# Talking-heads attention and a gated feed-forward: in each step, three blocks of four (two of three) go into the first head mixing as split fp32r pairs, instead of two (one)

## The chip, the cores and the metric

The kernel runs on one core of a Trainium2 chip. The metric is the time of one execution on the device in microseconds; the time given for a kernel is the median of several executions. The trace is that of one further execution, taken with the hardware profiler.

## The reference

```python
scores = scale * np.matmul(q, k.transpose(0, 1, 3, 2))      # batch 4, heads 12, seq 448, dim 64
scores = np.einsum('bhij,hg->bgij', scores, w_pre)          # first mixing of the heads
scores = scores - np.max(scores, axis=-1, keepdims=True)
attn = np.exp(scores)
attn = attn / (np.sum(attn, axis=-1, keepdims=True) + 1e-09)
attn = np.einsum('bhij,hg->bgij', attn, w_post)             # second mixing
out = np.matmul(attn, v).astype(np.float32)
...
h = x @ w_in                                                # x: (1792, 768), w_in: (768, 2048)
g = np.where(pos, h, np.where(neg, 0.0, (h + beta) ** 2 / (4.0 * beta)))
return (g @ w_out).astype(np.float32)
```

## The kernel before

The program has two parts. The attention fills the first half of the span, the feed-forward the second; the change touches only the attention.

**Tiles, blocks, groups.** The 448 query rows of a batch are cut into tiles of 120, 120, 120 and 88 rows, 16 tiles in all. `scores` writes the scores of a tile, for all 12 heads, to `ssb` (row, head, key). A block is 10 query rows times 12 heads, so 120 rows of 448 keys: `load_s` gathers it by a DMA from `ssb` into a tile `s` of its own (tag `s10`, 8 buffers). In this form the mixing of the heads is one matrix product with a 120x120 block-diagonal matrix. A tile of 120 rows has 12 blocks in 3 groups of four; the tile of 88 rows has 9 blocks in 3 groups of three. There are 48 groups and 180 blocks.

**A step.** The loop over n handles one group per step, and the order of each engine's work is the order of the code (there is no scheduler). In step n the code issues the loads of group n+1; `pre` of the blocks of group n (first mixing into a PSUM tile `ps_l`, on PE); `row_max` (DVE); the split of a block of the next group; `exps` (ACT, tile `e`); `norm` (DVE, then `wr` on POOL); the remaining splits; part of the conversion of the feed-forward's weights (`wt`, `wk` on ACT and DVE, an add on POOL); `post` of group n-1 (second mixing on PE into `ps_a`, which ACT copies to `aT`); in some steps the transposes of the next keys (`trans_k`, `ps_k`) and queries (`trans_q`, `ps_t`); `pv` (`ps_x`, copied to `xo`); the scores of a later tile (`ps_s`, copied to `ssb` by ACT and DVE); and further loads. The first of group n-1's `post` is written inside the loop of `exps`, ahead of the fourth; ACT copies the other three after it. Steps 0 to 47 are meant where a step is numbered.

**Two forms of the first mixing.** A block that was not split goes into `pre` as one fp32 product (line 200; the trace shows two instructions for one). A block that was split goes in as three fp32r products (line 198): high part with high weights, high with low, low with high. `split` makes the high part `sh` by a cast (DVE, line 187) and the low part `sl` by a subtraction (DVE, line 188).

**PSUM.** `ps_l`, `ps_a`, `ps_k`, `ps_t` (after the first tiles), `ps_x` and the second pair of `ps_s` all come from one pool of 6 buffers, which are handed out in turn: a new tile takes the buffer of the tile six before it, and PE waits until that one has been read.

**Loads.** All these loads are issued from SP's queue, in the order of the code. In a group of four they are issued as blocks 1, 3, 0, 2; in a group of three as 1, 0, 2.

Of the kernel before, what the change touches and what calls it, by code (L numbers as in the profile page):

```python
# [10 lines left out]
F32R = mybir.dt.float32r  # L11
# [3 lines left out]
AF = mybir.ActivationFunctionType  # L15
# [7 lines left out]
def tile_talking_heads_moe(  # L23
# [11 lines left out]
    nc = tc.nc  # L35
    B, H, S, D = q.shape
# [5 lines left out]
    KM = IB * H  # L42
# [17 lines left out]
    ap_ = s_att.enter_context(tc.tile_pool(name="att", bufs=2))  # L60
# [12 lines left out]
    for b in range(B):  # L73
        for i0 in range(0, S, QT):
            n = min(QT, S - i0)
            tiles.append((b, i0, n, -(-n // IB)))
    blocks = []
    groups = []
# [6 lines left out]
    NG = len(groups)  # L85
# [89 lines left out]
    def load_s(m):  # L175
        t, o, ni, c = blocks[m]
        n, nb = tiles[t][2:]
        x = ap_.tile([KM, S], F32, tag="s10", name="s10", bufs=8)
        nc.sync.dma_start(out=x[:ni * H], in_=ssb[t][o:n:nb])  # L179
        s10[m] = x  # L180

    def split(m):
        k = blocks[m][2] * H
        x = s10.pop(m)
        hi = ap_.tile([KM, S], F32R, tag="sh", name="sh", bufs=2)
        lo = ap_.tile([KM, S], F32R, tag="sl", name="sl", bufs=2)
        nc.vector.tensor_copy(out=hi[:k], in_=x[:k])
        nc.vector.tensor_tensor(out=lo[:k], in0=x[:k], in1=hi[:k].bitcast(F32), op=ALU.subtract)
        s10[m] = (hi, lo)

    def pre(m):

        k = blocks[m][2] * H
        lps[m] = ps_l.tile([KM, S], F32, tag="l", name="ps_l")
        x = s10.pop(m)
        if isinstance(x, tuple):
            for j, (w, y) in enumerate(((wpre_h, x[0]), (wpre_l, x[0]), (wpre_h, x[1]))):
                nc.tensor.matmul(out=lps[m], lhsT=w[:k], rhs=y[:k], start=(j == 0), stop=(j == 2))  # L198
        else:
            nc.tensor.matmul(out=lps[m], lhsT=wpre[:k], rhs=x[:k], start=True, stop=True)  # L200

    def row_max(m):
        nm = ap_.tile([KM, 1], F32, tag="nm", name="nm", bufs=8)
        nc.vector.tensor_reduce(out=nm, in_=lps[m], axis=AX.X, op=ALU.max, negate=True)  # L204
        lps[m] = (lps[m], nm)

    def exps(m, j, sm):
        ps, nm = lps.pop(m)
        e = ap_.tile([KM, S], F32, tag="e", name="e", bufs=8)
        nc.scalar.activation(out=e, in_=ps, func=AF.Exp, bias=nm, accum_out=sm[:, j:j + 1])  # L210
        ex[m] = e

    def norm(ms, sm):
        k = len(ms)
        rs = ap_.tile([KM, 4], F32, tag="rs", name="rs", bufs=3)
        nc.vector.tensor_scalar_add(out=rs[:, :k], in0=sm[:, :k], scalar1=1e-9)
        nc.vector.reciprocal(out=rs[:, :k], in_=rs[:, :k])  # L217
        for j, m in enumerate(ms):
            ni = blocks[m][2]
            w = ap_.tile([KM, H, IB], F32, tag="wr", name="wr", bufs=8)  # L220
            nc.gpsimd.tensor_scalar_mul(out=w[:, :, :ni], in0=wpost[:, :, :ni], scalar1=rs[:, j:j + 1])  # L221
            wr[m] = w

    def post(m):
        t, o, ni, c = blocks[m]
        if o == 0:
            aT[t] = ap_.tile([KP, KC, H, QT], F32, tag="aT", name="aT")
        ps = ps_l.tile([KP, KC, H * IB], F32, tag="l", name="ps_a")
        e, w = ex.pop(m), wr.pop(m)
        for r in range(KC):  # L230
            nc.tensor.matmul(out=ps[:, r, :ni * H], lhsT=e[:, r * KP:(r + 1) * KP],  # L231
                             rhs=w[:, :, :ni], start=True, stop=True)
        nc.scalar.activation(out=aT[t][:, :, :, c:c + ni],  # L233
                             in_=ps[:, :, :ni * H].rearrange("q r (h i) -> q r h i", h=H), func=AF.Copy)
# [242 lines left out]
    with tc.manual_schedule():  # L477
# [41 lines left out]
        for m in groups[0]:  # L519
# [7 lines left out]
            out=wpre.rearrange("p (i g) -> p i g", g=H),  # L527
# [3 lines left out]
            out=wpost, in0=wrep[:, 1, :].unsqueeze(2).to_broadcast([KM, H, IB]),  # L531
# [56 lines left out]
        def convs(goal):  # L588
            while conv and nconv - len(conv) < goal:
                conv.popleft()()  # L590

        for n in range(NG + 2):
            if n == NE:
                s_qk.close()
                pool['fp'] = ctx.enter_context(tc.tile_pool(name="ffn", bufs=2, side="right",
                                                            reuse_waits="tile"))
                pool['ps_h'] = ctx.enter_context(tc.tile_pool(
                    name="ps_h", bufs=2, space=PSUM, side="right", reuse_waits="tile"))
            if n == NG - 1:
                s_ss.close()  # L600
                pool['fw'] = ctx.enter_context(tc.tile_pool(name="ffw", bufs=2, side="right",
                                                            reuse_waits="tile"))
            share = nconv / (NE - 1)
            ms = groups[n] if n < NG else ()
            old = list(groups[n - 1]) if 0 < n <= NG else []
            if n + 1 < NG:
                for m in (*groups[n + 1][1::2], *groups[n + 1][::2]):
                    load_s(m)
            if ms:
                sm = ap_.tile([KM, 4], F32, tag="sm", name="sm", bufs=3)  # L610
            for m in ms:
                pre(m)
            nxt = list(groups[n + 1][1::2]) if n + 1 < NG else []
            for m in ms:
                row_max(m)
            if nxt:
                split(nxt.pop(0))
            for j, m in enumerate(ms):
                if j == 3:
                    post(old.pop(0)) if old else None  # L620
                exps(m, j, sm)
            if ms:
                norm(ms, sm)
            for m in nxt:
                split(m)
            convs(share * (n + 0.4))
            for m in old:
                post(m)
            for f in at.pop(n, ()):
                f()  # L630
            for t, g in vis2.pop(n, ()):
                pv(t, g)
            for f in [scores(t, hps) for t, hps in vis.pop(n, ())]:
                f()
            for f in late.pop(n, ()):
                f()
            convs(share * (n + 1))
            if n == NG:
                h = ffn1(0)
# [77 lines left out]
```

## Time and profile before

| | |
|---|---|
| median of the runs | 946.18 us (944.99 to 948.36) |
| the profiled execution | 944.17 us |
| its span in the trace | 942.4 us |
| mean granted TensorE clock | 0.998 |
| PE matmul busy | 926.5 us, 98% |
| DVE / ACT / POOL busy | 609.4 / 542.2 / 179.7 us |

The span runs from the first to the last instruction; the time of the execution has 1.8 us more. A busy share is a mean over both parts of the program, whose limits differ.

### The profile page before, as it was taken

What the parts mean: (1) busy time and instruction counts of PE and PEld (TensorE: products, weight loads), DVE (VectorE), ACT (ScalarE), POOL (GpSimd) and SP (SyncE); (2) the same over time, 40 slices, a digit from 0 to 9 for tenths busy, and PEclk for the clock granted to TensorE, in tenths of its full rate; (3) what the DMA queues carried; (4) which work ended last, traced back from release to release, by engine and by line L of the source; (5) the groups of instructions that cost most, each with busy time, mean ns of one, the idle gap of its engine ahead of it and who ended that gap; (6) DMA issues with size and microseconds to landing.
All of it is one profiled execution on the core that took longest, in us unless ns stands there. A gap on an engine that the chain in (4) does not pass through costs nothing.

```text
span 942.4 us, 17968 instructions
## 1 busy us (share of the span) xinstructions
PE 926.5 (98%) x6734; PEld 781.4 (83%) x6734; DVE 609.4 (65%) x1113; ACT 542.2 (58%) x1146; POOL 179.7 (19%) x253
## 2 busy tenths in 40 slices
PE   7989999999999999999999999999999999999998
PEld 6668888888887888888888888888888888888997
DVE  4678768787778868765556675655445555445774
ACT  4767777766786777776655563533334433334553
POOL 0243334342434234331202230000000000000000
PEclk9999999999999999999999999999999999999999
DMA  6966756776678756744554540210000200000100
GB/s 110 235 194 182 209 177 207 244 207 178 200 220 221 214 169 205 221 171 145 153 196 151 184 140 1 76 37 1 12 12 12 85 1 1 11 1 20 55 1 34
DMA packets 118362, 115.21 MB, mean 122 GB/s; under 512 B 61701, under 2 KB 107269, under 8 KB 118277
## 3 DMA queue, kind: packets, MB, share of 16 engines
q1 hardware_dynamic: 115492, 113.38, 40.0%
q10 hardware_dynamic: 2784, 0.69, 0.5%
q8 instruction: 54, 0.88, 0.4%
q14 instruction: 32, 0.25, 0.1%
HBM read 55.85 MB, written 19.66 MB: 80 GB/s over the span
## 4 chain that ended last, share of the span: by engine, by line
PE 95%; DMA 3%; SPq 1%; DVE 0%; ACT 0%; issue 0%
PE o L458 25%; PE ps_h L419 25%; PE ps_a L231 15%; PE ps_x L247 9%; PE ps_l L200 8%; PE ps_s L155 6%; PE ps_l L198 5%; DMA s<-ssb 2%; PE ps_t L138 1%; PE ps_k L121 1%; DMA qraw<-in_q_dram 1%; SPq L179 0%; DMA k<-in_k_dram 0%; DVE kl L128 0%; SPq L110 0%; SPq L101 0%
## 5 line engine op out<-in xcount | busy, mean ns | idle before, releaser
L221 POOL TENSOR_SCALAR wr<-wpost,rs 120x120 f32<-120x120 f32 x180 | 113.3, 645 | 304.5 <-DVE rs L217 257.0
L231 PEld LDWEIGHTS ps_a<-wr,e 120*112 120x112 f32 x1440 | 154.3, 177 | 6.7 <-issue 4.9
L231 PE MATMUL ps_a<-wr,e 120*112 120x120 f32 (+1 forms) x1440 | 155.2, 266 | 0.0
L210 ACT ACTIVATE e<-ps_l,nm 120x448 f32<-120x448 f32 x180 | 112.8, 632 | 54.6 <-DVE nm L204 54.0
L419 PE MATMUL ps_h<-xh,wil 128*128 128x512 f32 (+1 forms) x384 | 139.5, 363 | 0.0
L419 PE MATMUL ps_h<-xl,wih 128*128 128x512 f32 (+1 forms) x384 | 139.2, 362 | 0.0
L419 PE MATMUL ps_h<-xh,wih 128*128 128x512 f32 (+1 forms) x384 | 139.2, 362 | 0.0
L458 PE MATMUL o<-woh,gh 128*128 128x512 f32 (+1 forms) x444 | 114.6, 339 | 0.0
L458 PE MATMUL o<-wol,gh 128*128 128x512 f32 (+1 forms) x444 | 114.1, 339 | 0.0
L433 ACT ACTIVATE a<-ps_h,c 128x512 f32<-128x512 f32 (+1 forms) x64 | 40.6, 634 | 127.6 <-PE ps_h L419 127.5
L458 PE MATMUL o<-woh,gl 128*128 128x512 f32 (+1 forms) x444 | 114.0, 338 | 0.0
L434 DVE TENSOR_TENSOR mx<-ps_h,a 128x512 f32<-128x512 f32 (+1 forms) x64 | 40.0, 625 | 110.4 <-ACT a L433 110.3
L204 DVE TENSOR_REDUCE nm<-ps_l 120x1 f32<-120x448 f32 x180 | 104.1, 619 | 10.5 <-PE ps_l L200 8.0
L200 PE MATMUL ps_l<-s,wpre 120*120 120x448 f32 x196 | 94.7, 567 | 6.4 <-DMA s<-ssb 6.4
L233 ACT ACTIVATE aT<-ps_a 112x480 f32<-112x480 f32 x180 | 95.8, 590 | 2.4 <-PE ps_a L231 2.1
L437 ACT ACTIVATE gh<-mx 128x512 fp32r<-128x512 f32 (+1 forms) x63 | 36.6, 581 | 90.3 <-DVE mx L435 90.3
L458 PEld LDWEIGHTS o<-woh,gl 128*128 128x128 f32 x444 | 75.0, 189 | 11.5
L247 PE MATMUL ps_x<-aT,v 112*64 112x120 f32 (+1 forms) x1536 | 83.8, 262 | 0.0
L458 PEld LDWEIGHTS o<-wol,gh 128*128 128x128 f32 x444 | 75.5, 188 | 9.9
L458 PEld LDWEIGHTS o<-woh,gh 128*128 128x128 f32 x444 | 75.7, 188 | 9.6
L419 PEld LDWEIGHTS ps_h<-xl,wih 128*128 128x128 f32 x384 | 72.4, 189 | 12.1
L419 PEld LDWEIGHTS ps_h<-xh,wih 128*128 128x128 f32 x384 | 72.4, 189 | 11.5
(83 smaller groups left out, 1459.1 us busy)
## 6 DMA issues: line engine op xcount, KB each, us to landing
s<-ssb SPq DMA_DIRECT2D x172, 210.0 KB
wraw<-in_moe_w_in_dram SPq DMA_DIRECT2D x32, 384.0 KB
raw<-in_moe_w_out_dram SPq DMA_DIRECT2D x20, 384.0 KB
wid<-wt SPq DMA_DIRECT2D x32, 192.0 KB
wi<-wid SPq DMA_DIRECT2D x16, 384.0 KB
v<-in_v_dram SPq DMA_DIRECT2D x12, 448.0 KB
out_dram<-osb SPq DMA_DIRECT2D x14, 384.0 KB
wraw<-in_moe_w_out_dram SPq DMA_DIRECT2D x12, 384.0 KB
```

Of the source, the lines that this page charges most:

```text
L155: nc.tensor.matmul(out=ps[s][:n], lhsT=qt[t][x][r, hp, :n], rhs=kt[b, hp][y][r, :], start=(m == 0), stop=(m == 2))
L198: nc.tensor.matmul(out=lps[m], lhsT=w[:k], rhs=y[:k], start=(j == 0), stop=(j == 2))
L200: nc.tensor.matmul(out=lps[m], lhsT=wpre[:k], rhs=x[:k], start=True, stop=True)
L204: nc.vector.tensor_reduce(out=nm, in_=lps[m], axis=AX.X, op=ALU.max, negate=True)
L210: nc.scalar.activation(out=e, in_=ps, func=AF.Exp, bias=nm, accum_out=sm[:, j:j + 1])
L221: nc.gpsimd.tensor_scalar_mul(out=w[:, :, :ni], in0=wpost[:, :, :ni], scalar1=rs[:, j:j + 1])
L231: nc.tensor.matmul(out=ps[:, r, :ni * H], lhsT=e[:, r * KP:(r + 1) * KP], rhs=w[:, :, :ni], start=True, stop=True)
L233: nc.scalar.activation(out=aT[t][:, :, :, c:c + ni], in_=ps[:, :, :ni * H].rearrange("q r (h i) -> q r h i", h=H), func=AF.Copy)
L247: nc.tensor.matmul(out=ps[s * D:(s + 1) * D, m, :n], lhsT=vt[b, g][:, 2 * m + s, r * D:(r + 1) * D], rhs=a[:, r, 4 * g + 2 * m + s, :n], s ...
L419: nc.tensor.matmul(out=ps[:, :n], lhsT=w[:, kk, :], rhs=x[:, :n], start=(c == 0), stop=(c == last))
L433: nc.scalar.activation(out=a[:, :n], in_=ps[:, :n], func=AF.Relu, scale=0.5, bias=c05)
L458: nc.tensor.matmul(out=o[bank][:, c0:c0 + ne], lhsT=g[:, t * 128:(t + 1) * 128], rhs=w[:, e0:e0 + ne], start=(f == 0 and m == 0 and c0 == ...
```

## The change

The blocks that are split are now all of a group but its first: blocks 1, 2 and 3 of four (before: 1 and 3), blocks 1 and 2 of three (before: 1). The low part no longer has a tile of its own but is written over the scores in their `s` buffer; `sh` has 4 buffers instead of 2. Block 3's cast is issued from ACT instead of DVE, its subtraction stays on DVE. The loads are issued as blocks 1, 2, 3, 0 (of three: 1, 2, 0), so block 0, the one that goes into the fp32 product, comes last. Group 0 is mixed without splits in both kernels.

```diff
-    def split(m):
+    def split(m, act=False):
         k = blocks[m][2] * H
         x = s10.pop(m)
-        hi = ap_.tile([KM, S], F32R, tag="sh", name="sh", bufs=2)
-        lo = ap_.tile([KM, S], F32R, tag="sl", name="sl", bufs=2)
-        nc.vector.tensor_copy(out=hi[:k], in_=x[:k])
+        hi = ap_.tile([KM, S], F32R, tag="sh", name="sh", bufs=4)
+        lo = x.bitcast(F32R)
+        if act:
+            nc.scalar.activation(out=hi[:k], in_=x[:k], func=AF.Copy)
+        else:
+            nc.vector.tensor_copy(out=hi[:k], in_=x[:k])
         nc.vector.tensor_tensor(out=lo[:k], in0=x[:k], in1=hi[:k].bitcast(F32), op=ALU.subtract)
...
-                for m in (*groups[n + 1][1::2], *groups[n + 1][::2]):
+                for m in (*groups[n + 1][1:], groups[n + 1][0]):
                     load_s(m)
...
-            nxt = list(groups[n + 1][1::2]) if n + 1 < NG else []
+            nxt = list(groups[n + 1][1:]) if n + 1 < NG else []
...
+            if nxt:
+                split(nxt.pop(0))
             for m in nxt:
-                split(m)
+                split(m, act=True)
```

On PE, the first mixing of group 2 (step 2), from the last product of the scores ahead of it to the second mixing behind it. The number of an `s` tile rises in the order in which the loads are issued. Before:

```order
L155 MATMUL ps_s_519<-kl_201,qh 120x448
L200 MATMUL ps_l<-s_425,wpre 120x448
L198 MATMUL ps_l<-sh,wpre_h 120x448
L198 MATMUL ps_l<-sh,wpre_l 120x448
L198 MATMUL ps_l<-sl,wpre_h 120x448
L200 MATMUL ps_l<-s_427,wpre 120x448
L198 MATMUL ps_l<-sh,wpre_h 120x448
L198 MATMUL ps_l<-sh,wpre_l 120x448
L198 MATMUL ps_l<-sl,wpre_h 120x448
L231 MATMUL ps_a<-wr,e 112x120 x16
```

The same place of the changed kernel:

```order
L155 MATMUL ps_s_523<-kl_201,qh 120x448
L203 MATMUL ps_l<-s_428,wpre 120x448
L201 MATMUL ps_l<-sh,wpre_h 120x448
L201 MATMUL ps_l<-sh,wpre_l 120x448
L201 MATMUL ps_l<-s_422,wpre_h 120x448
L201 MATMUL ps_l<-sh,wpre_h 120x448
L201 MATMUL ps_l<-sh,wpre_l 120x448
L201 MATMUL ps_l<-s_424,wpre_h 120x448
L201 MATMUL ps_l<-sh,wpre_h 120x448
L201 MATMUL ps_l<-sh,wpre_l 120x448
L201 MATMUL ps_l<-s_426,wpre_h 120x448
L234 MATMUL ps_a<-wr,e 112x120 x16
```

The third block's fp32 product has become three fp32r ones, and the tile that PE needs first is the fourth that is loaded (`s_428` of 422, 424, 426, 428) where it was the third (`s_425` of 421, 423, 425, 427).

On ACT, step 7, from its exponentials to the copy of `ps_x`. Before:

```order
L210 ACTIVATE e,sm<-ps_l,nm 120x448 x3
L233 ACTIVATE aT<-ps_a 112x48x10
L210 ACTIVATE e,sm<-ps_l,nm 120x448
L282 ACTIVATE wt<-wraw 128x384
L288 ACTIVATE wk<-wraw 128x384
L233 ACTIVATE aT<-ps_a 112x48x10 x3
L140 ACTIVATE qh<-ps_t 128x360
L254 ACTIVATE xo<-ps_x 128x240
```

The same place of the changed kernel:

```order
L213 ACTIVATE e,sm<-ps_l,nm 120x448 x3
L236 ACTIVATE aT<-ps_a 112x48x10
L213 ACTIVATE e,sm<-ps_l,nm 120x448
L188 ACTIVATE sh<-s_1234 120x448
L285 ACTIVATE wt<-wraw 128x384
L291 ACTIVATE wk<-wraw 128x384
L236 ACTIVATE aT<-ps_a 112x48x10 x3
L140 ACTIVATE qh<-ps_t 128x360
L257 ACTIVATE xo<-ps_x 128x240
```

The cast of the next group's block 3 stands between the last exponential and the conversions and copies behind it; `s_1234` is the third of the four tiles loaded in that step.

## Rows read from the trace of the kernel before

**Rows 1.** The page: busy time, and the chain that ended last.
```profile
PE 926.5 (98%) x6734; PEld 781.4 (83%) x6734; DVE 609.4 (65%) x1113; ACT 542.2 (58%) x1146; POOL 179.7 (19%) x253
...
PE 95%; DMA 3%; SPq 1%; DVE 0%; ACT 0%; issue 0%
```

**Rows 2.** Busy time by step: stretch, length, PE, PEld, DVE, ACT, POOL, clock, DMA.
```profile
90.55:101.02 10.47, 10.47 (x100) 8.70 (x98) 9.23 (x20) 7.58 (x20) 3.37 (x5) 1.00 0.81 232
...
314.04:324.50 10.46, 10.46 (x99) 8.69 (x97) 8.37 (x19) 7.58 (x20) 3.29 (x5) 1.00 0.86 232
...
sum 410.88, PE 410.88 PEld 339.49 DVE 307.59 ACT 299.04 POOL 149.31; mean PE 9.13 PEld 7.54 DVE 6.84 ACT 6.65 POOL 3.32
```

**Rows 3.** Timeline of PE, second half of step 8's first mixing: start, duration.
```profile
102.48 0.91 PE L200 MATMUL ps_l<-s,wpre 120*120 120x448 f32 x2
102.88 0.72 PE L198 MATMUL ps_l<-sh,wpre_h 120*120 120x448 f32 x1
103.43 0.36 PE L198 MATMUL ps_l<-sh,wpre_l 120*120 120x448 f32 x1
103.64 0.37 PE L198 MATMUL ps_l<-sl,wpre_h 120*120 120x448 f32 x1
103.84 3.44 PE L231 MATMUL ps_a<-wr,e 120*112 120x120 f32 x32
```

**Rows 4.** Groups by line: the subtractions of the splits, ACT's copies of scores.
```profile
L188 DVE TENSOR_TENSOR sl<-s,sh 120x448 fp32r<-120x448 f32 (+1 forms) x82 | 54.2, 661 | 2.8
...
L160 ACT ACTIVATE ssb<-ps_s 120x448 f32<-120x448 f32 (+1 forms) x96 | 52.1, 546 | 23.3 <-PE ps_s L155 19.9 <-DMA s<-ssb 0.4
```

**Rows 5.** Timeline of PE: start and end of step 3's first mixing, start of step 46.
```profile
51.77 1.82 PE L200 MATMUL ps_l<-s,wpre 120*120 120x448 f32 x2 [4.49 <-DMA s<-ssb]
...
55.84 0.37 PE L198 MATMUL ps_l<-sl,wpre_h 120*120 120x448 f32 x1
...
449.49 0.98 PE L200 MATMUL ps_l<-s,wpre 120*120 120x448 f32 x2
```

**Rows 6.** Timeline of DVE: casts of steps 2, 6, 7, 31 (both), 39 and 45.
```profile
49.67 0.39 DVE L187 CAST sh<-s 120x448 fp32r<-120x448 f32 x1 [5.94 <-DMA s<-ssb]
...
84.19 0.40 DVE L187 CAST sh<-s 120x448 fp32r<-120x448 f32 x1 [0.35 <-DMA s<-ssb]
...
94.95 0.40 DVE L187 CAST sh<-s 120x448 fp32r<-120x448 f32 x1 [0.65 <-DMA s<-ssb]
...
319.67 0.39 DVE L187 CAST sh<-s 120x448 fp32r<-120x448 f32 x1 [1.89 <-DMA s<-ssb]
...
320.93 0.36 DVE L187 CAST sh<-s 120x448 fp32r<-120x448 f32 x1
...
392.65 0.39 DVE L187 CAST sh<-s 120x448 fp32r<-120x448 f32 x1 [1.92 <-DMA s<-ssb]
...
448.40 0.39 DVE L187 CAST sh<-s 120x448 fp32r<-120x448 f32 x1 [3.29 <-DMA s<-ssb]
```

**Rows 7.** Busy time and clock at the start of step 3.
```profile
51.74:54.50 2.76, 2.73 (x5) 1.77 (x6) 2.73 (x6) 0.00 (x0) 2.76 (x5) 0.50 0.65 242
```

**Rows 8.** Timeline of SP's queue: the loads that step 31 issues.
```profile
314.53 3.44 SPq L179 DMA_DIRECT2D s<-ssb  x4
```

**Rows 9.** Timeline of ACT, step 31: behind the last exponential.
```profile
319.19 0.58 ACT L282 ACTIVATE wt<-wraw 128x384 f32<-128x384 f32 x1
319.63 0.59 ACT L288 ACTIVATE wk<-wraw 128x384 int32<-128x384 uint32 x1
320.08 1.54 ACT L233 ACTIVATE aT<-ps_a 112x480 f32<-112x480 f32 x3
```

**Rows 10.** Timeline of PE, step 31: the product with the values.
```profile
321.32 1.86 PE L247 MATMUL ps_x<-aT,v 112*64 112x120 f32 x32
```

## The prediction

> **What bounds the kernel now.** I read the page first: PE is busy 98% and the chain that ended last is PE for 95% [rows 1]. A busy matmul row proves little, so the second view is busy time by step. I cut the attention at the first product of each step, from 51.77 us on; in all 45 stretches PE is busy for the whole length (410.88 of 410.88 us), while DVE has 307.59 and ACT 299.04 [rows 2]. So from about 60 us on a microsecond taken off PE is a microsecond off the time, as long as the other engines stay ahead of it. Ahead of that the chain goes through the loads of `s`: step 3 begins at 51.77 after PE had waited 4.49 us for one [rows 5]. The third view is DVE's timeline: the first cast of a step often waits for its load [rows 6]. That is the only supply that is nearly late, and the change touches it.
>
> **What the change gives PE.** 82 splits become 129: 35 steps whose next group has four blocks and 12 with three each get one more, 47 in all. Each turns an fp32 product into three fp32r products. In step 8 the fp32 product starts at 102.48 and its fp32r block has ended when the second mixing starts at 103.84; successive fp32r products start 0.205 us apart (103.43, 103.64, 103.84) [rows 3]. So an fp32r block takes 3 x 0.205 = 0.615, the fp32 one 1.36 - 0.615 = 0.745, and a swap saves 0.13 to 0.14; I take 0.135. Of the 47 groups concerned, 1 and 2 are mixed before step 3, whose start a load sets, and 3 falls into the stretch below; the other 44 give 44 x 0.135 = **-5.9 us**.
>
> **What is added elsewhere.** DVE gets 47 subtractions of 0.66 us [rows 4], and 12 casts of 0.39 [rows 6]; ACT gets 35 casts, about 0.5 us of its queue each (bounds: 0.44 for the 384 elements between two conversions [rows 9] and 0.55 for a copy of 448 [rows 4]). Step 7 is among DVE's fullest: 9.23 of 10.47 us [rows 2] becomes 9.9 of 10.3. That still fits, so DVE's busy time costs nothing by itself; if it did not fit, each such step would lose what overhangs. The Trainium skill, page "ScalarE: Activation LUTs", section "What ACT_TABLE_LOAD costs", gives 186 ns + 0.833 ns per element, less some 93 ns of overlap, for such an ACTIVATE: an estimate of 0.47 us for 448 elements. The trace's 0.546 us for a whole copy agrees, and the sum by the page would be about 0.3 us lower.
>
> **Block 0 is loaded last.** This costs where PE waits for loads. At step 3 the first load of the group landed by 49.67 (DVE had waited for it [rows 6]) and the third at 51.77 [rows 5]: 1.05 us per load. The fourth lands at about 52.75, so PE starts 1.0 us later. Before, the mixing ended at 55.84 + 0.205 = 56.05. The first 2.76 us run at a granted clock of 0.50, the 1.2 GHz level, after PE's wait [rows 7]; an fp32 and an fp32r block fill them (2 x 1.36 = 2.72), two more at full clock take 1.23, and the mixing ends at about 56.7: **+0.65 us**. At step 46 the first load was there at 448.40 after 3.29 us of waiting [rows 6] and PE began at 449.49 [rows 5] with the second. Now it needs the third: 448.4 + 1.9 to 2.1 = 450.3 to 450.5: **+0.9 us**. Elsewhere it costs nothing: in step 31, where the first load is late, the fourth lands 2.6 to 3.2 us behind it, by 322.9 [rows 6], and PE wants it at 324.50 [rows 2].
>
> **ACT's cast stands in front of the copies that PE needs.** ACT works in order. Behind the last exponential it now waits for the third load, casts, and only then does the conversions and the three copies of `ps_a` to `aT`. Until the first of these is done, one PSUM buffer is not free. Counted from the code, with six buffers in turn: in a step with `ps_k` and `ps_t`, that buffer is the one of `ps_x`; in a step with `ps_t` alone, the second `ps_s` of the last pair; otherwise, the next step's first `ps_l`.
>
> Step 31 is the plainest. Its first load is there at 319.64 [rows 6]. The loads are issued 0.86 us apart [rows 8] and landed 1.05 apart at step 3, so the third is 1.7 to 2.1 us behind; I take 1.9. Cast done 319.64 + 1.9 + 0.5 = 322.04; two conversions, 0.9 [rows 9]: 322.94; first copy, 0.55: 323.5. PE would want the buffer at 321.32 - 0.135 = 321.2 [rows 10]. It waits 2.3 us. Step 7 has the same shape and starts at 90.55 [rows 2], so `ps_x` is due at 97.83 - 0.135; its first load is there at 94.92 [rows 6], the copy done at 98.77: 1.1 us. Done for every step whose next group has four blocks, this leaves eight more with a wait, steps 6 (cast at 84.19) to 39 (392.65) [rows 6], of 0.1 to 0.8 us each, 3.1 together. Sum 6.5. Where such steps follow each other (6 and 7, 30 and 31, 27 and 28, 38 and 39) the first wait gives the loads of the next some lead, for which I take 0.8 off: **+5.7 us**. With 1.7 instead of 1.9 the sum is about 4, with 2.1 about 8.
>
> The sum is -5.9 + 0.65 + 0.9 + 5.7 = +1.35 us. Against the profiled execution's own 944.17 us that is 945.5; the median of the runs shown is 2.0 us higher, so I say **947.5 us**, no change that can be told (a measurement of this kernel tells 0.3%, 2.8 us, from none).
>
> **The rivals.**
> *The gain comes through.* If the loads of a group land close together, ACT hardly waits: in step 31 DVE's second cast, at 320.93, shows no wait, so the second load was at most 1.3 us behind the first [rows 6]. Then only the casts themselves delay the copies, and with a third load less than 1 us behind the first, step 31 would still lose 1.4 and the others little: -5.9 + 0.65 + 0.4 + 1.5 = -3.35, and with nothing lost at steps 3 and 46 -4.4: 942 to 943 us. It speaks against it that the loads are issued 0.86 us apart.
> *ACT falls behind and PE pays in many steps.* The same wait, with its lag carried on: ACT's later exponentials delay the row sums, these POOL's `wr` and its add, and this the store that stands ahead of the next loads in SP's queue, so the loads themselves become later. With the third load 2.1 us behind, the waits alone are 8 us; half a microsecond more in the ten steps makes 13. Then -5.9 + 1.55 + 8 to 13 = +3.7 to +8.7: 950 to 955. It decides once the waits pass 7.2 us. For it speaks that steps 7 and 31 run DMA at 0.81 and 0.86 [rows 2]; against it that ACT has some 2 us to spare in such a step.
> The Trainium skill, page "TensorE: Matmul & The Clock Gate", the table at its head, says that ACT's queue of 8 is strictly first in, first out. By that rule the copies cannot pass the waiting cast; DVE's 1.89 us wait with work behind it [rows 6] agrees.
> *DVE becomes the bound* in the steps with `ps_k`: it would show as PE waiting for DVE's copies; at 9.9 of 10.3 us I give it no share of its own but count it with the slow rival.
>
> **Chances.** No change 0.43; the gain comes through 0.25; slower 0.32. The first case by itself, waits of 4 to 7.2 us, is 945.8 to 949. The range goes from the fast rival's 942, less 0.5 for the spread of a measurement, to the middle of the slow one, 952.5.
>
> **What would show it.** In the trace after: 98 fp32 first mixings fall to 51, and the first mixing of a four-group step is 0.135 us shorter (right). PE waits of 1 to 2.5 us for ACT's `aT` ahead of `ps_x` in steps 7 and 31, and waits of ACT's cast for `s` (right); no such waits: the first rival. PE's start of step 3 near 52.7. Wrong would be the whole if PE waited for DVE's splits ahead of line 201, or if the steps without a wait did not get shorter.

## The result and the profile after

| | before | after |
|---|---|---|
| median of the runs | 946.18 us (944.72 to 948.36) | 950.2 us (947.57 to 953.77) |
| ratio, with its 95% interval | | 1.0054 (1.0040 to 1.0069) |
| the profiled execution / its span | 944.17 / 942.4 us | 950.07 / 948.3 us |
| fp32 / split first mixings | 98 / 82 | 51 / 129 |

By the ratio the changed kernel is about 5 us slower. The ratio is not the quotient of the two medians, which is 1.0042 (4.0 us) and also lies in the interval. A second set of runs of the same kernel, beside later experiments, gave 1.0062 (1.0044 to 1.0080).

The page of the changed kernel, in the lines that answer to [rows 1]:

```profile
PE 923.3 (97%) x6781; PEld 792.0 (84%) x6781; DVE 637.6 (67%) x1172; ACT 549.6 (58%) x1181; POOL 193.8 (20%) x253
...
PE 86%; DMA 7%; ACT 2%; DVE 2%; SPq 1%; issue 1%; ACTq 0%; DVEq 0%
```

PE has 3.2 us less to do and the span is 5.9 us longer. The chain that ended last, 95% PE before, goes through PE for 86% and through DMA for 7%. So PE got the shorter work and now waits. Busy time by stretch (as [rows 2]): step 7, step 31, and steps 4 to 43 together:

```profile
91.42:101.97 10.55, 10.38 (x100) 8.86 (x99) 9.74 (x21) 8.14 (x21) 3.83 (x5) 1.00 0.88 226
316.46:327.42 10.96, 10.38 (x100) 8.87 (x98) 10.07 (x22) 8.14 (x21) 3.83 (x5) 1.00 0.95 239
60.24:435.58 375.34, 369.38 (x3531) 315.85 (x3529) 309.29 (x659) 280.88 (x714) 149.81 (x196) 1.00 0.65 195
```

Before, PE was busy for the whole of every such stretch. Now 5.96 of 375.34 us are idle, and DVE is at 10.07 of 10.96 us in step 31.

Timeline of PE in step 8, answering to [rows 3]; it starts at 101.97, and 104.66 is the second mixing:

```profile
101.97 1.01 PE L203 MATMUL ps_l<-s,wpre 120*120 120x448 f32 x2
102.47 0.71 PE L201 MATMUL ps_l<-sh,wpre_h 120*120 120x448 f32 x1
...
104.25 0.37 PE L201 MATMUL ps_l<-sh,wpre_l 120*120 120x448 f32 x1
104.45 0.36 PE L201 MATMUL ps_l<-s,wpre_h 120*120 120x448 f32 x1
104.66 2.11 PE L234 MATMUL ps_a<-wr,e 120*112 120x120 f32 x19
```

Three split blocks follow one fp32 block; from the second of their nine products on they start 0.205 us apart. The step lasts 10.03 us (101.97 to 112.00) where it lasted 10.16: the swap gives its 0.13 us wherever nothing waits.

The groups by line of the two engines that got the work ([rows 4] has the subtractions of before): busy and mean ns, then the idle time ahead and what ended it.

```profile
L188 ACT ACTIVATE sh<-s 120x448 fp32r<-120x448 f32 x35 | 20.4, 582 | 34.3 <-DMA s<-ssb 34.1
...
L191 DVE TENSOR_TENSOR s<-s,sh 120x448 fp32r<-120x448 f32 x129 | 83.7, 660 | 6.6 <-ACT sh L188 2.7
```

ACT's 35 casts wait 34.1 us in all for loads. What that does to PE is seen in three steps. ACT in steps 6, 12 and 31, the cast and the copies to `aT` behind it (the last in answer to [rows 9]):

```profile
86.70 0.58 ACT L188 ACTIVATE sh<-s 120x448 fp32r<-120x448 f32 x1 [0.87 <-DMA s<-ssb]
...
87.63 1.48 ACT L236 ACTIVATE aT<-ps_a 112x480 f32<-112x480 f32 x3
...
145.64 0.58 ACT L188 ACTIVATE sh<-s 120x448 fp32r<-120x448 f32 x1 [3.70 <-DMA s<-ssb]
146.12 0.98 ACT L236 ACTIVATE aT<-ps_a 112x432 f32<-112x432 f32 x2
...
322.25 0.58 ACT L188 ACTIVATE sh<-s 120x448 fp32r<-120x448 f32 x1 [0.19 <-DMA s<-ssb]
```

and PE in the same steps, in answer to [rows 10]:

```profile
88.23 1.86 PE L250 MATMUL ps_x<-aT,v 112*64 112x120 f32 x32 [0.73 <-ACT aT L236]
...
146.69 1.01 PE L203 MATMUL ps_l<-s,wpre 120*120 120x448 f32 x2 [1.02 <-ACT aT L236]
...
324.25 1.86 PE L250 MATMUL ps_x<-aT,v 112*64 112x120 f32 x32 [0.58 <-ACT aT L236]
```

In step 6 the cast waits 0.87 us, the copies start at 87.63, and PE's `ps_x` begins 0.73 us late at 88.23. In step 12 the third load comes 3.3 us behind the first (for which DVE's first cast, the first line below, had waited), and it is the next step's first `ps_l` that lacks a buffer. In step 31 the cast itself waits only 0.19 us; there the exponentials start late, behind late row maxima: 1.85 us into the step (second line; it starts at 316.46) where they began 1.53 into it before (third line; 314.04).

```profile
142.36 0.39 DVE L190 CAST sh<-s 120x448 fp32r<-120x448 f32 x1 [1.93 <-DMA s<-ssb]
...
318.31 2.21 DVE L207 TENSOR_REDUCE nm<-ps_l 120x1 f32<-120x448 f32 x4
...
315.57 2.21 DVE L204 TENSOR_REDUCE nm<-ps_l 120x1 f32<-120x448 f32 x4
```

The other loss is at the end of the attention, whose groups of three have no cast on ACT. PE at the start of steps 3 and 46 (as [rows 5]), DVE's first cast in step 45 (as [rows 6]), and the clock at steps 46 and 3 (as [rows 7]):

```profile
52.57 0.98 PE L203 MATMUL ps_l<-s,wpre 120*120 120x448 f32 x2 [3.04 <-DMA s<-ssb]
...
55.22 2.01 PE L234 MATMUL ps_a<-wr,e 120*112 120x120 f32 x18
...
454.24 1.82 PE L203 MATMUL ps_l<-s,wpre 120*120 120x448 f32 x2 [3.31 <-DMA s<-ssb]
```

```profile
451.74 0.39 DVE L190 CAST sh<-s 120x448 fp32r<-120x448 f32 x1 [5.22 <-DMA s<-ssb]
```

```profile
454.24:457.30 3.06, 3.06 (x6) 2.04 (x7) 1.88 (x4) 0.49 (x1) 1.61 (x2) 0.50 0.85 245
...
52.57:55.33 2.76, 2.76 (x13) 2.17 (x14) 2.72 (x7) 2.76 (x7) 2.67 (x3) 1.00 0.66 241
```

Step 46 began 4.75 us later than before (1.58 of that was there when step 45 began), with a wait of 3.31 us and then 3 us at 0.50, the 1.2 GHz level. Step 3 began at 52.57, 0.80 later than before, but at full clock.

**Where the time went, by stretch.** I cut every trace at the first product of each step's first mixing and took its lengths less those of before. In the trace of the changed kernel the start (up to step 5) is +0.36 us, steps 5 to 43 are +1.14, steps 44 to 46 +4.57, the rest -0.17; sum 5.9. Steps 5 to 43 hold 39 swaps, worth -5.27, so 6.41 us of waits stand against them (called waits below). In 14 steps ACT's cast waited over 0.6 us. Seven of them (6, 12, 15, 18, 23, 27, 39) have 5.4 of the 6.4 us. The other seven (11, 14, 24, 26, 35, 36, 38) lost 0.03 us at most, though the cast waited 1.28 to 2.45 us in them. ACT in step 36:

```profile
369.85 0.58 ACT L188 ACTIVATE sh<-s 120x448 fp32r<-120x448 f32 x1 [2.45 <-DMA s<-ssb]
```

This cast starts 7.48 us into its step, that of step 12, with the same copies behind it, 8.73. In step 36 PE does not wait for `aT`. So a wait of the cast costs PE only what is left of it when PE wants the buffer.

### The profile page after: what moved, and what is told of

Same layout as the page of the kernel before. It is cut to its first block, busy times and chain, and to the rows that moved or that the text cites. A ratio compares the mean times of both kernels' runs of the same rounds, so it can differ in the third digit from the quotient of the medians.

```text
span 948.3 us, 18180 instructions
## 1 busy us (share of the span) xinstructions
PE 923.3 (97%) x6781; PEld 792.0 (84%) x6781; DVE 637.6 (67%) x1172; ACT 549.6 (58%) x1181; POOL 193.8 (20%) x253
## 4 chain that ended last, share of the span: by engine, by line
PE 86%; DMA 7%; ACT 2%; DVE 2%; SPq 1%; issue 1%; ACTq 0%; DVEq 0%
PE o L461 25%; PE ps_h L422 24%; PE ps_a L234 11%; PE ps_x L250 7%; PE ps_l L201 7%; DMA s<-ssb 6%; PE ps_s L155 6%; PE ps_l L203 4%; SPq L179 1%; PE ps_t L138 1%; DMA qraw<-in_q_dram 1%; ACT e L213 1%; ACT aT L236 1%; DVE ssb L164 0%; DMA k<-in_k_dram 0%
## 5 line engine op out<-in xcount | busy, mean ns | idle before, releaser
L224 POOL TENSOR_SCALAR wr<-wpost,rs 120x120 f32<-120x120 f32 x180 | 127.0, 720 | 293.4 <-DVE rs L220 226.2
L207 DVE TENSOR_REDUCE nm<-ps_l 120x1 f32<-120x448 f32 x180 | 102.1, 618 | 8.2 <-PE ps_l L203 6.3
L236 ACT ACTIVATE aT<-ps_a 112x480 f32<-112x480 f32 x180 | 93.5, 582 | 1.7 <-PE ps_a L234 1.6
L191 DVE TENSOR_TENSOR s<-s,sh 120x448 fp32r<-120x448 f32 x129 | 83.7, 660 | 6.6 <-ACT sh L188 2.7
```

The source lines that it names most:

```text
L236: nc.scalar.activation(out=aT[t][:, :, :, c:c + ni], in_=ps[:, :, :ni * H].rearrange("q r (h i) -> q r h i", h=H), func=AF.Copy)
```

## The experiments

Ratios are to the kernel before on the same chip, with 95% intervals. The columns on the right are from one trace of each kernel, against the trace of before; waits are the difference in steps 5 to 43 plus 0.135 us for each swap there (39; 32 in the selective kernel; none with two splits). A row is one execution: the two traces of the changed kernel differ by 5.8 us in the waits and by 3.3 at the end, the profiled execution of "all casts on DVE" (942.77 us) is the fastest of its 11, and that of "load order only" (948.96) is among the slowest of its 12. So prices are taken from the ratios, and the rows say where time goes.

| kernel | ratio (interval) | start | steps 5 to 43 | waits in them | steps 44 to 46 |
|---|---|---|---|---|---|
| after | 1.0054 (1.0040 to 1.0069) | +0.36 | +1.14 | 6.4 | +4.57 |
| after, again | 1.0062 (1.0044 to 1.0080) | +1.01 | +6.97 | 12.2 | +1.24 |
| low part in place only | 1.0001 (0.9993 to 1.0010) | +0.12 | +0.16 | 0.2 | +0.55 |
| load order only | 1.0018 (1.0008 to 1.0028) | +2.01 | +1.98 | 2.0 | +0.70 |
| two splits, ACT casts block 3 | 1.0075 (1.0057 to 1.0093) | -1.03 | +6.55 | 6.6 | +2.14 |
| all casts on DVE | 0.9994 (0.9982 to 1.0007) | -0.25 | -2.09 | 3.2 | +1.11 |
| ACT's cast behind the copies | 1.0042 (1.0029 to 1.0054) | +1.79 | +2.63 | 7.9 | +1.19 |
| ACT casts the first load | 1.0088 (1.0070 to 1.0105) | +1.56 | +7.20 | 12.5 | +1.41 |
| block 3 loaded first | 1.0127 (1.0091 to 1.0163) | +0.81 | +12.90 | 18.2 | +1.80 |
| subtraction on POOL | 1.0097 (1.0081 to 1.0113) | +2.73 | +6.71 | 12.0 | +0.20 |
| old order at the end | 1.0039 (1.0027 to 1.0051) | +1.62 | +1.73 | 7.0 | -0.16 |
| fp32 block last | 0.9979 (0.9970 to 0.9987) | +0.47 | -0.43 | 4.8 | +0.54 |
| fp32 last, selective | 0.9978 (0.9968 to 0.9988) | -0.29 | -0.98 | 3.3 | -0.07 |

**All casts on DVE.**

```diff
             for m in nxt:
-                split(m, act=True)
+                split(m)
```

> The third block's cast goes back from ACT to DVE; splits, load order and in-place low part stay as in the change. Theory A (ACT's cast, waiting for the third load in front of the copies to aT, is what takes back the gain between steps 5 and 43): PE's waits for ACT's aT there, 6.5 us in the trace of the change, fall below 1 us, and the time is 944 us (943 to 945.5); the start and the end of the attention stay as late as in the change. Rival (DVE's load is the limit): DVE gets 35 casts of 0.39 us more, PE waits for DVE's copies instead, and the time stays at 949 to 952 us.

Measured: 944.5 us, ratio 0.9994, as theory A said: 5.7 us less than the changed kernel by the ratios, and level with the kernel before. But 3.2 us of waits are left. Steps 19 and 31 have 0.7 each, with waits of PE for `aT` of 0.64 and 0.63 us, where less than 1 us in all was expected. There DVE is late, as its first row maximum in step 31 (the step starts at 312.60) and then ACT and PE show:

```profile
315.33 2.21 DVE L207 TENSOR_REDUCE nm<-ps_l 120x1 f32<-120x448 f32 x4
```

```profile
316.04 0.63 ACT L213 ACTIVATE e<-ps_l,nm 120x448 f32<-120x448 f32 x1 [2.35 <-DVE nm L207]
```

```profile
320.49 1.86 PE L250 MATMUL ps_x<-aT,v 112*64 112x120 f32 x32 [0.63 <-ACT aT L236]
```

DVE came out of step 30 with work left, so the maxima start 2.73 us into the step (1.53 in the same step of before, 1.85 in the changed kernel), and `aT` is late without any wait for a load in ACT's queue. In step 26 PE waits for block 0, which is now loaded last:

```profile
274.46 0.98 PE L203 MATMUL ps_l<-s,wpre 120*120 120x448 f32 x2 [0.83 <-DMA s<-ssb]
```

**Two splits, with ACT's cast.**

```diff
-            nxt = list(groups[n + 1][1:]) if n + 1 < NG else []
+            nxt = list(groups[n + 1][1::2]) if n + 1 < NG else []
...
-            if nxt:
-                split(nxt.pop(0))
             for m in nxt:
                 split(m, act=True)
```

> The change, with the old number of splits: blocks 1 and 3 of four, block 1 of three. Block 3's cast stays on ACT, the load order is the new one; DVE does one cast and two subtractions in a step, so less than before the change. PE loses the 44 swaps again, so steps 5 to 43 are compared with those of before. Theory A (ACT's cast and its wait for the third load are the cause by themselves): PE's waits in steps 5 to 43 stay near 6 us, and the time is 954 to 957 us. Rival (DVE's added casts and subtractions, which run over into the next step and delay the row maxima and with them the exponentials and ACT's copies, are the larger part): the waits fall below 2.5 us, and the time is 949 to 951 us, of which 4 to 5 us stand at the end of the attention.

Measured: 952.73 us, ratio 1.0075, a little below the range of theory A; the waits are 6.6 us, as theory A said, with less work on DVE than before the change. Step 27 shows it, on ACT and then on PE:

```profile
287.18 0.58 ACT L188 ACTIVATE sh<-s 120x448 fp32r<-120x448 f32 x1 [2.75 <-DMA s<-ssb]
...
288.11 1.02 ACT L236 ACTIVATE aT<-ps_a 112x480 f32<-112x480 f32 x2
```

```profile
288.72 0.46 PE L155 MATMUL ps_s<-kh,qh 64*120 64x448 f32 x1 [1.16 <-ACT aT L236]
```

**The load order only,** in the kernel before:

```diff
-                for m in (*groups[n + 1][1::2], *groups[n + 1][::2]):
+                for m in (*groups[n + 1][1:], groups[n + 1][0]):
```

> The kernel before with the load order alone: 1, 2, 3, 0 of four and 1, 2, 0 of three; splits and casts as before. Theory B (block 0 last makes PE wait where loads are late): the end of the attention (steps 44 to 46) loses 1 to 4.5 us, the start 0 to 1, single steps in between (12, 24, 26, 36) some tenths each, 1 to 1.5 together: 948 to 951 us. Rival (the order costs nothing by itself; the end was late because the three-block groups had lost their lead to ACT and DVE): 945 to 946.5 us.

Measured: 947.47 us, ratio 1.0018, so 1.7 us: less than theory B's 2 to 5, more than nothing. Its trace has 2.0 us of waits in steps 5 to 43, most of them in steps 14, 26 and 28. PE at the end of step 28, where it waits for a load:

```profile
297.87 0.98 PE L200 MATMUL ps_l<-s,wpre 120*120 120x448 f32 x2 [0.45 <-DMA s<-ssb]
```

With the changed kernel and the two kernels above this makes a square, in ratios: two splits 1.0018 (DVE casts) and 1.0075 (ACT casts block 3); three splits 0.9994 and 1.0054. The first of the four still has a tile of its own for the low part, which the next run shows to be worth nothing. ACT's cast costs 0.0057 with two splits and 0.0060 with three, 5.4 to 5.7 us. The third split gives 0.0024 or 0.0021, 2.0 to 2.3 us, not 5.9. Each such difference is uncertain by about 0.002, 2 us. That the two prices of ACT's cast agree makes them firmer; that the two of the third split agree follows from the same four numbers and is no second check.

**The low part in place only,** in the kernel before:

```diff
-        hi = ap_.tile([KM, S], F32R, tag="sh", name="sh", bufs=2)
-        lo = ap_.tile([KM, S], F32R, tag="sl", name="sl", bufs=2)
+        hi = ap_.tile([KM, S], F32R, tag="sh", name="sh", bufs=4)
+        lo = x.bitcast(F32R)
```

> The kernel before with one part of the change alone: the low part is written over the scores, and sh has 4 buffers; splits, load order and casts are those of before. Theory A and B: in-place writing costs nothing, 946 us (945.5 to 947), PE's waits as before. Rival (a buffer that PE instead of DVE releases makes the loads late): casts wait longer for their loads and the time is 948 us or more.

Measured: 945.46 us, ratio 1.0001. That PE now releases the `s` buffers costs nothing, to 0.9 us, with the splits and the load order of before.

**ACT's cast behind the copies.**

```diff
-            for m in nxt:
-                split(m, act=True)
             convs(share * (n + 0.4))
             for m in old:
                 post(m)
+            for m in nxt:
+                split(m, act=True)
```

> The third block's cast stays on ACT but is issued behind the conversions and the three copies to aT. Theory A: the waits for aT go (6.5 us), but DVE's third subtraction now waits for a later cast, and with it DVE's copies of keys and scores, which gives back 1 to 2 us: 945 to 946 us. Rival (the waits for aT come from PE's and POOL's own order, not from the cast): no change, 950 us.

Measured: 949.07 us, ratio 1.0042; 3 to 4 us over theory A. The interval overlaps that of the changed kernel, so no change in the time can be told, as the rival had it, but not for its reason. The waits did not go, they moved: to steps 7, 8, 19, 20, 31 and 32, 0.6 to 0.8 us each, and to 12 and 23. DVE in step 7:

```profile
101.18 0.62 DVE L191 TENSOR_TENSOR s<-s,sh 120x448 fp32r<-120x448 f32 x1 [1.35 <-ACT sh L188]
101.72 0.62 DVE L125 CAST kh<-ps_k 128x448 fp32r<-128x448 f32 x1
```

DVE stands 1.35 us in front of the keys for the cast that is now late, and carries it into the next step.

**ACT casts the first load.**

```diff
-            if nxt:
+            four = len(nxt) == 3
+            if nxt and not four:
                 split(nxt.pop(0))
...
-            if nxt:
-                split(nxt.pop(0))
+            if four:
+                split(nxt.pop(0), act=True)
             for m in nxt:
-                split(m, act=True)
+                split(m)
```

> ACT keeps one cast in each step whose next group has four blocks, at the same place in its queue, but it casts the block that is loaded first; DVE casts the second and the third. So ACT has the same work in front of the copies to aT and waits for the first load instead of the third. Theory A with the wait as its main part: PE's waits in steps 5 to 43 fall from 6.4 us to 2 to 4 us, and the time is 944.5 to 947 us. Rival (the cast itself in front of the copies is enough, whatever it waits for): the waits stay at 6 us and the time at 950 us.

Measured: 954.61 us, ratio 1.0088; outside both ranges. ACT in step 6 has no wait ahead of its cast, yet everything is late; then DVE in the same step:

```profile
85.04 0.63 ACT L213 ACTIVATE e<-ps_l,nm 120x448 f32<-120x448 f32 x1 [2.41 <-DVE nm L207]
...
87.95 0.59 ACT L188 ACTIVATE sh<-s 120x448 fp32r<-120x448 f32 x1
```

```profile
88.11 0.17 DVE L219 TENSOR_SCALAR rs<-sm 120x4 f32<-120x4 f32 x1 [1.57 <-ACT e L213]
```

The edit also took the first split out of the gap in which DVE waits for the exponentials. DVE is idle there for 1.57 us, does all its work on the three blocks (three subtractions, two casts) behind the row sums, and starts the next maxima late. So this run doesn't separate the wait from the cast; it shows that the gap is worth a split.

**Block 3 loaded first,** the same question with that split kept in the gap:

```diff
-                for m in (*groups[n + 1][1:], groups[n + 1][0]):
+                for m in (*groups[n + 1][3:], *groups[n + 1][1:3], groups[n + 1][0]):
...
-                split(nxt.pop(0))
+                split(nxt.pop(), act=len(nxt) == 1)
             for m in nxt:
-                split(m, act=True)
+                split(m)
```

> The change with block 3 loaded first (order 3, 1, 2, 0): ACT casts it at the same place as in the change, and its load has long landed by then; DVE splits block 1 ahead of the row sums as in the change (now the second load), and behind them subtracts block 3 and splits block 2 (now the third load). DVE thus has one cast and one subtraction less in front of the wait for the third load than in the experiment with ACT casting block 1, and keeps its place ahead of the row sums. Theory A with the wait for the third load as its main part: PE's waits in steps 5 to 43 fall from 6.4 us (12.2 in the second trace) to 2 to 4, and the time is 944.5 to 947 us. Rival (the cast itself, about 0.5 us in front of the copies, or DVE's added work behind it is enough): the waits stay at 5 us or more, and the time at 949 to 952 us.

Measured: 957.19 us, ratio 1.0127; worse than either expected. The longest waits are in steps 12, 13, 24, 28, 36, 37 and 40. From step 11 to step 13, on DVE, POOL, SP, ACT and PE:

```profile
133.99 0.39 DVE L190 CAST sh<-s 120x448 fp32r<-120x448 f32 x1 [1.31 <-DMA s<-ssb]
...
135.16 0.17 DVE L220 RECIPROCAL rs<-rs 120x3 f32<-120x3 f32 x1
```

```profile
135.53 2.58 POOL L224 TENSOR_SCALAR wr<-wpost,rs 120x120 f32<-120x120 f32 x3 [6.62 <-DVE rs L220]
138.09 1.99 POOL L304 TENSOR_TENSOR wt<-wt,wk 128x384 int32<-128x384 int32 x2
```

```profile
139.12 0.34 SPq L333 DMA_DIRECT2D wod<-wt  x1
...
140.03 4.01 SPq L179 DMA_DIRECT2D s<-ssb  x4
```

```profile
145.53 0.58 ACT L188 ACTIVATE sh<-s 120x448 fp32r<-120x448 f32 x1 [2.92 <-DMA s<-ssb]
```

```profile
148.63 1.27 PE L203 MATMUL ps_l<-s,wpre 120*120 120x448 f32 x2 [2.60 <-DMA s<-ssb]
```

DVE's first split now waits for the second load, in front of the row sums. `rs` is late, so are POOL's `wr` and its adds, and SP, which had stood 4.8 us for the add's `wt`, stores it at 139.12 and issues the next loads at 140.03: 2.75 us into step 12 (it starts at 137.28), against 1.58 in the changed kernel (136.91) and 1.25 before (136.52). The loads of these two, the changed kernel first:

```profile
138.49 3.42 SPq L179 DMA_DIRECT2D s<-ssb  x4
...
137.77 3.42 SPq L179 DMA_DIRECT2D s<-ssb  x4
```

Even the first load then comes late (145.53). Here a late load made the loads behind it later.

**The subtraction on POOL,** all casts on DVE:

```diff
-        if act:
-            nc.scalar.activation(out=hi[:k], in_=x[:k], func=AF.Copy)
-        else:
-            nc.vector.tensor_copy(out=hi[:k], in_=x[:k])
-        nc.vector.tensor_tensor(out=lo[:k], in0=x[:k], in1=hi[:k].bitcast(F32), op=ALU.subtract)
+        nc.vector.tensor_copy(out=hi[:k], in_=x[:k])
+        (nc.gpsimd if third else nc.vector).tensor_tensor(out=lo[:k], in0=x[:k], in1=hi[:k].bitcast(F32), op=ALU.subtract)
...
             for m in nxt:
-                split(m, act=True)
+                split(m, third=True)
```

> All casts on DVE, and the third block's subtraction on POOL instead of DVE, which takes 0.66 us out of DVE's step; the rest as in the change. If DVE's overrun in the steps with transposes of keys is what was left of the waits (0.7 us each in steps 19 and 31 with all casts and subtractions on DVE), these waits go, and the time is 943 us (942 to 944). Rival (POOL's subtraction, 1 to 1.5 us in order behind the scaling of the weights, delays its add and the stores and loads behind it): 945 to 948 us.

Measured: 954.33 us, ratio 1.0097; the rival's direction, and worse than its range. One subtraction takes 1152 ns on POOL (mean of 35) against 660 on DVE, in front of POOL's adds, and in five steps PE itself waits for it, 1.6 us in all.

```profile
L188 POOL TENSOR_TENSOR s<-s,sh 120x448 fp32r<-120x448 f32 x35 | 40.3, 1152 | 0.0
```

**The old order at the end.** Groups 45 to 47 are loaded and split as before the change:

```diff
-                for m in (*groups[n + 1][1:], groups[n + 1][0]):
+                g = groups[n + 1]
+                for m in ((*g[1:], g[0]) if n + 1 < NG - 3 else (*g[1::2], *g[::2])):
...
-            nxt = list(groups[n + 1][1:]) if n + 1 < NG else []
+            nxt = list(groups[n + 1][1:] if n + 1 < NG - 3 else groups[n + 1][1::2]) if n + 1 < NG else []
```

> The last three groups (45 to 47, three blocks each) are loaded in the old order and split as before; all else as in the change. Theory B (at the end PE waits for the last load of the group because block 0 comes last): steps 45 and 46 lose 1 to 1.5 us instead of 4.5, less 0.4 for three swaps undone: 946.5 to 947 us. Rival (the loads of these groups are issued late, whatever their order, since the low part holds the buffers or since PE is already behind): at most 1 us gained, 949 to 950 us.

Measured: 949.25 us, ratio 1.0039, in the rival's range. Still, steps 44 to 46 are as long as before (-0.16), so what is lost there does hang on these two lines. By the ratios that is 1.4 to 2.2 us (the intervals overlap), not the 4.6 of the first trace.

**The fp32 block last,** all casts on DVE. The first mixing, the maxima, the exponentials and the second mixing go through the blocks as 1, 2, 3, 0:

```diff
-            ms = groups[n] if n < NG else ()
-            old = list(groups[n - 1]) if 0 < n <= NG else []
+            ms = (*groups[n][1:], groups[n][0]) if n < NG else ()
+            old = [*groups[n - 1][1:], groups[n - 1][0]] if 0 < n <= NG else []
...
             for m in nxt:
-                split(m, act=True)
+                split(m)
```

> All casts on DVE as in the experiment of that name, and in each step the block that stays fp32 is mixed last (blocks 1, 2, 3, 0 in the first mixing, the row maxima, the exponentials and the second mixing), so that PE wants the loads in the order in which they come. Theory B: what remained at the end (1.1 us) and the waits for block 0's load in steps 12, 24, 26 and 36 (about 1.4 us) go, and the time is 942 us (941 to 943). Rival (PE now waits for DVE's split of block 1 at the start of a step, or the waits only move): 944 to 946 us.

Measured: 943.56 us, ratio 0.9979, faster than both kernels, and between the two expected ranges. The end is on time to 0.5 us, but steps 13 and 25 lose 1.5 each. DVE, then PE there:

```profile
144.53 0.39 DVE L190 CAST sh<-s 120x448 fp32r<-120x448 f32 x1 [1.22 <-DMA s<-ssb]
...
147.54 0.52 DVE L141 TENSOR_TENSOR ql<-ps_t,qh 128x360 fp32r<-128x360 f32 x1
```

```profile
148.12 1.01 PE L203 MATMUL ps_l<-s,wpre 120*120 120x448 f32 x2 [0.84 <-DVE ql L141]
```

DVE waits 1.22 us for the second load, `ql`, which reads a PSUM buffer, stands behind the splits, and PE waits for that buffer: the pattern that ACT had, now on DVE.

**The same, selective:** in every sixth step only two blocks are split.

```diff
-            nxt = list(groups[n + 1][1:]) if n + 1 < NG else []
+            nxt = list(groups[n + 1][1:3 if n % 6 == 0 else 4]) if n + 1 < NG else []
```

> As the kernel in which the fp32 block is mixed last and all casts are on DVE, but in every sixth step (0, 6, 12, ... 42) the next group has only two blocks split. These are the steps in which the third load came late (12, 24) or after which DVE ran over into the next step (18, 30). Theory A in its second part (what is left are waits for late third loads and DVE's overrun in these steps): steps 13 and 25 lose their 1.5 us each, 19, 31 and 37 their 1.2 together, for eight swaps given up, 1.1 us: 940.5 to 942 us. Rival (the waits move to other steps, since the loads stay late): 943 to 944.5 us.

Measured: 942.72 us, ratio 0.9978, between the two expected ranges. Steps 19 and 31 lost their waits, 13 and 25 kept most (1.0 and 1.1), and a wait of 0.9 came in step 28; with eight swaps given up it is level with the one before it. Some 0.2% against the kernel before is what this way gives.

**The changed kernel, again,** with no edit.

> The changed kernel, profiled a second time on this chip. If the excess over the shorter steps is a property of the program, the sum of PE's waits in steps 5 to 43 is again 6 to 7 us and the end of the attention (steps 44 to 46) again 4 to 5 us late. If the end's 4.6 us were the arrival of a few loads in one execution, the end is late by 0.5 to 2.5 us only; the time is 950 us either way.

Measured: 951.54 us, ratio 1.0062. The end is late by 1.24 us this time, as the second case said, but steps 5 to 43 have 12.2 us of waits where 6 to 7 were expected. The profiled execution took 953.21 us, near the longest of its runs, as the first (950.07) was near the median. Step 6 has the same shape as in the first trace, a little larger; ACT, then PE:

```profile
87.49 0.58 ACT L188 ACTIVATE sh<-s 120x448 fp32r<-120x448 f32 x1 [0.98 <-DMA s<-ssb]
```

```profile
89.03 1.86 PE L250 MATMUL ps_x<-aT,v 112*64 112x120 f32 x32 [0.86 <-ACT aT L236]
```

So which steps lose how much differs from one execution to the next, and the runs of this kernel spread over 6 us (947.5 to 953.8) where those of before, beside the two sets, spread over 3.6 (944.7 to 948.4) and 2.6 (944.2 to 946.8).

## Why the prediction came out as it did

The forecast was 947.5 us and no change; the kernel is 0.54% slower, inside the range, but above the 945.8 to 949 us of the case held likeliest and on the side of the second rival. By its terms:

- **The swaps.** Right: 0.13 to 0.15 us in every step without a wait, 51 fp32 first mixings left.
- **Step 3.** PE's start was put at 52.75 and was 52.57. The mixing was to end at 56.7, since I carried the half clock of [rows 7] over; the clock stayed at full and it ended at 55.22. Step 4 then lost 1.2 us (1.09 of it a wait of PE for late exponentials), which I had not seen. Up to step 5 the forecast comes to +0.5 (0.65 less the swap of step 4) and was +0.36 in one trace, +1.01 in the other.
- **The end.** Forecast +0.9, less three swaps +0.5; measured +4.57 and +1.24. The mechanism is right (the old order there brings it to -0.16), but the first load itself was late in the first trace (DVE's first cast at 451.74, 448.40 before), and the sum had held it fixed.
- **The waits behind ACT's cast.** That ACT's cast costs time is shown: with it there are 6.4 us of waits or more with two splits and with three, without it 2.0 and 3.2, and the price is 5.4 to 5.7 us by the ratios. That it costs it through the copies is read from the trace, where PE waits 4.8 us in all for `aT`; the cast behind the copies did not give the time back. The sum was forecast as 5.7, and that it fits is luck. The steps behind it were wrong: steps 31 and 7, for which I had worked out 2.3 and 1.1, lost 0.64 and 0.21, so the waits of 1 to 2.5 us that were to show it did not come; steps 28, 30 and 38, which I had named, lost 0.06 at most; and steps 12 and 23, which I had not named, 1.1 and 1.2. The failed step is that each group's first load comes when it came before and the third 1.9 us behind. In 11 of the 14 steps in which both casts waited, the distance was 1.8 to 1.9; in step 27 it was 2.4, in steps 12 and 23 3.3 to 3.4, and the first loads had moved.
- **DVE costs nothing by itself.** This failed. I checked that its work fits in the step (9.9 of 10.3 us), and not that it has to be done by the time the row maxima are due. In the changed kernel the maxima of step 31 start 0.3 us late; with all casts on DVE it runs over in steps 19 and 31, and the third split is worth 2.0 to 2.3 us by the ratios instead of 5.9.
- **The load order elsewhere.** Put at nothing, since step 31 had room. This failed too: the trace of the order alone has 2.0 us of waits in steps 5 to 43, and in steps 26 and 28 PE waits 0.32 and 0.45 us for a load.

Along the ratios (load order alone +1.7 us, third split on DVE -2.3, its cast moved to ACT +5.7) the change comes to +5.1 us. The forecast had +1.35: for start and end, which the order sets, +1.55, and for ACT +5.7, both right in size, if not in place; and for the third split -5.9, the swaps alone, since DVE's added work was put at nothing. The swaps came, and the third split still gave 3.6 us less than that, which also turned the side of the result. So the step that failed is that the third split costs nothing beside the swaps as long as DVE's work fits. In the trace with all casts on DVE 1.5 us of waits stand in steps 19 and 31, where DVE is late (and it has one cast more there than in the change). The rest isn't placed, and no run tells what of it is DVE's and what comes of loads that are late for a faster PE.

The second rival had named a way from late loads to still later ones through `rs`, `wr`, the add and the store; the run with block 3 first shows the links from `rs` on, though there `rs` was late because a split waited in front of it and not because of late exponentials. How much of the changed kernel's own loss runs that way stays open, as does the split of ACT's 5.5 us between the wait and the cast's 0.48 us: the two runs that were to separate them moved DVE's work as well. The traces speak for the wait (5.4 of 6.4 us stand in steps where the cast waited; in steps 7, 19 and 30 of the first trace, as full as any but with a wait of 0.08 us at most, PE lost 0.2 us at most), but that is read, not tested.

The Trainium skill, page "TensorE: Matmul & The Clock Gate", the table at its head, calls ACT's and DVE's queues strictly first in, first out. The trace agrees: in step 12 PE was through with `ps_a` at 142.16 and began `ps_x` at 142.39, and the copies to `aT` began at 146.12, behind the cast that waited 3.70 us.

## What to carry to other kernels

An instruction that waits for a transfer should not stand, on an in-order engine, ahead of the copies that give the matrix engine its PSUM buffers back; look for it before counting its own 0.5 us. Moving it behind them did not help here, since another engine waited for its result; taking it off that engine did. An engine's busy share says that work fits into a step, not that it is done by the moment when the next engine wants it: ask what is due first in the next step, and use the gaps in which the engine waits anyway. Where supply is nearly late, load in the order in which the blocks are wanted, or want them in the order in which they come: mixing the last-loaded block last, with the casts on DVE, turned a loss of 0.5% into a gain of 0.2% (the casts give most of it; the order of mixing adds 0.15%, with intervals that overlap).

## What the runs showed of the hardware

- After a wait of 3.04 us at step 3 the granted clock was 1.00; after waits of 3.31 us at step 46, and of 4.49 at step 3 of before, the next 2.8 to 3.1 us ran at 0.50, the 1.2 GHz level.
- Loads issued 0.86 us apart landed 1.8 to 1.9 us apart over two loads in 11 of the 14 steps in which it can be read, 2.4 in step 27 and 3.3 to 3.4 in steps 12 and 23; in the run with block 3 first, a load issued at 140.03 was there at 145.5.
- A subtraction of 120x448 elements took 1152 ns on POOL and 660 on DVE; a cast of the same size 582 on ACT and 379 on DVE.
